# Retention and expert layer on one core: gate matrices loaded by feature, zero products in three gaps

## The chip, the core and the metric

The kernel runs on one core of a Trainium2 chip. The metric is device time in microseconds (us) from start to end of the program; the time before is 446.6 us, the median of three runs (444.99, 446.60 and 446.89 us). A core has five instruction streams that run side by side and wait for each other by semaphores: TensorE (PE) for matrix products, VectorE (DVE), ScalarE (ACT), GpSimd (POOL) and SyncE (SP), which here only issues DMAs.

## The reference

```python
# q, k, v: (4, 8, 768, 64); x of the second part: 3072 tokens x 512 features, 8 experts, F = 1024
state = gamma * state + einsum('bhd,bhe->bhde', k[:, :, t], v[:, :, t])     # for each token t
y[:, :, t] = einsum('bhd,bhde->bhe', q[:, :, t], state) / sqrt(64)
x = y.transpose(0, 2, 1, 3).reshape(3072, 512)
logits = x @ w_gate;  e_idx = argmax(logits, axis=1);  probs = softmax(logits)
eom = 1 / (1 + exp(-(x @ w_output_gate)))
for e in range(8):                                     # each token goes to one expert
    out[e_idx == e] = probs[., e] * eom[., e] * (relu(x[.] @ w1[e]) @ w2[e])
```

Two gate matrices of 512 features by 8 experts are read by the change: `w_gate`, which picks the expert, and `w_output_gate`.

## The kernel before

**Two phases.** The first takes the 3072 tokens in 24 chunks of 128 (four sequences of six), turns them into outputs of the retention, computes their logits, and scatters each token's row into a DRAM buffer sorted by expert. The second runs the experts over that buffer. In the last chunks of the first phase and behind it the largest expert's first 256 rows ("head") are worked off too.

**Order of the work.** In the first phase the order of the instructions of TensorE, VectorE, ScalarE and GpSimd is the order in which they are written; SyncE's DMA queue is ordered by a planner, which mostly keeps the written order. In the second phase TensorE and GpSimd keep the written order.

**A chunk i** (loop L666, `attend` L314) issues on SyncE the loads of key and value chunks i+3 (`load_k`, `load_v`) and, in even chunks, of a query pair (`load_q`); GpSimd scales the value chunk i+2 (`prep_v`, L281, three buffers). TensorE then runs: the scores `s` (L331, 16 products); the product of queries with the state (`py<-qt,sd`, L348; not in a sequence's first chunk); then `between()`: in even chunks from 2 on the logits of the two chunks before (`logits`, L379, which reads `wg`), the transposes of the keys of chunk i+1 (`kt_block`, `pk`, L286), in chunk 1 `spread_gates` (L255), the transposes of the queries of chunk i+2 (`qt_block`, `pq`, L304), and routing; then the products of masked scores with values (`py<-am,vs`, L353) and the state's update (`st`, L361). ScalarE copies the state out as `sd` (L365), VectorE masks the scores into `am` (L335). Key chunks have four buffers: `load_k(i+3)` waits until chunk i-1 has used its buffer.

**The gate matrices.** `wg` is 128 partitions by 4 groups by 32 columns: partition p of group g holds feature 128 g + p, with the two halves of 64 features swapped in groups 2 and 3; columns 0 to 7 belong to `w_gate`, 8 to 15 to `w_output_gate`. GpSimd clears `wg` at the start (L233). ScalarE's queue loads both matrices into `wgs` as 8 rows of 4 KB (L123), ahead of the load of `gv` (L125). In chunk 1, `spread_gates` multiplies them by an identity: 8 products, each shown as two instructions, put them into PSUM by feature, and six copies on VectorE (L257, L259) put them into `wg`. The first reader is `logits(0)` in chunk 2.

**Zero products.** `warm_up(ps, n)` (L138) issues n products of a 128x128 with a 128x512 tile of zeros in bf16; 14 of them stand at the start (L206). The PSUM tiles `pw`, `pg` (decays), `po` (gates) and `misc` (logits) share one buffer.

Of the kernel before, what the change touches and what calls it, by code (L numbers as in the profile page):

```python
# [10 lines left out]
F32 = mybir.dt.float32  # L11
# [21 lines left out]
def retention_moe_kernel(  # L33
# [14 lines left out]
    nc = tc.nc  # L48
    P = 128
    B, H, S, D = q.shape  # L50
    E, DM, DF = w1.shape
# [3 lines left out]
    NG = H // 2  # L55
# [8 lines left out]
    cpool = ctx.enter_context(tc.tile_pool(name="cpool", bufs=1))  # L64
# [53 lines left out]
    nc.scalar.dma_start(dqs, dec_q)  # L118
    dcs = cpool.tile([2, NC * NG], F32, name="dcs")
    nc.scalar.dma_start(dcs, dec_c)  # L120
    wgs = cpool.tile([2 * NG, P * E], F32, name="wgs")
    for j, w in enumerate((w_gate, w_ogate)):
        nc.scalar.dma_start(wgs[j * NG:j * NG + NG], w.rearrange("(g p) e -> g (p e)", p=P))  # L123
    gv = cpool.tile([P, NC, H], F32, name="gv")
    nc.scalar.dma_start(gv, dec_v)  # L125

# [11 lines left out]
    def warm_up(ps, n):  # L138
        for _ in range(n):
            nc.tensor.matmul(ps, wz[:, 0:P], wz, start=True, stop=True)  # L140
# [52 lines left out]
    with ExitStack() as actx:  # L193
# [22 lines left out]
        def load_v(i):  # L216
            b, c = divmod(i, NC)
            vn[i] = ap.tile([P, H, D], F32, name="vn", tag="vn", bufs=4)
            nc.sync.dma_start(vn[i], v[b, :, c * P:(c + 1) * P, :].rearrange("h p d -> p h d"))
# [27 lines left out]
                nc.vector.tensor_copy(gc[:, :, 2 * x:2 * x + 2],  # L247
                                      pm[:, x * NC * NG:(x + 1) * NC * NG].rearrange("p (c g) -> p c g", g=NG)[:, :, 2 * x:2 * x + 2])

        def spread_gates():  # L250

            po = ps_1.tile([P, 512], F32, name="po", tag="misc")[:, 0:2 * NG * E].rearrange("p (e j) -> p e j", e=E)
            wv = wgs.rearrange("j (p e) -> j p e", e=E)
            for e in range(E):
                nc.tensor.matmul(po[:, e], wv[:, :, e], ident[0:2 * NG, 0:2 * NG], start=True, stop=True)  # L255
            for j in range(2):
                nc.vector.tensor_copy(wg[:, 0:2, j * E:j * E + E].rearrange("p g e -> p e g"), po[:, :, j * NG:j * NG + 2])  # L257
                for h in range(2):
                    nc.vector.tensor_copy(wg[h * D:h * D + D, 2:4, j * E:j * E + E].rearrange("p g e -> p e g"),  # L259
                                          po[(1 - h) * D:(2 - h) * D, :, j * NG + 2:j * NG + 4])  # L260

        def more_gq(c):
            nc.gpsimd.tensor_mul(gq[:, c], gq[:, 0],
# [19 lines left out]
        def kt_block(i):  # L283
            pk = ps_t.tile([P, NG, P], F32, name="pk", tag="t")
            for g in range(NG):
                nc.tensor.transpose(pk[:, g], kn[i][:, 2 * g:2 * g + 2].rearrange("p h d -> p (h d)"), ident)  # L286
            kt[i] = ap.tile([P, NG, P], F32, name="kt", tag="kt", bufs=2)
            nc.scalar.copy(kt[i], pk)
# [3 lines left out]
        def qr_block(t):  # L292
            n, r = divmod(t, 2)
            qrs[t] = ap.tile([P, H, D], F32, name="qr", tag="qr", bufs=2)
            (nc.vector.tensor_copy if n == 0 else nc.scalar.copy)(qrs[t], qn[n][:, :, r * D:(r + 1) * D])
# [18 lines left out]
        def attend(i, between, before_state):  # L314
            b, c = divmod(i, NC)
            n, h2 = divmod(i, 2)
            own = slice(64 * h2, 64 * h2 + 64)

            def rm(t):
                return t.rearrange("p (r m) -> p r m", r=2)  # L320

            def qc(r, g):
                return qt[n][r, g, :, own]

            pss = []
            for hh in range(2):
                pss.append(ps_s.tile([P, NG, P], F32, name=f"s{hh}", tag="s"))
            for g in range(NG):
                for hh in range(2):
                    r = slice(hh * 64, hh * 64 + 64)  # L330
                    nc.tensor.matmul(rm(pss[hh][:, g]), kt[i][r, g], qc(r, g), start=True, stop=True)  # L331
            am = []
            for hh in range(2):
                a = ap.tile([P, NG, P], F32, name=f"am{hh}", tag=f"am{hh}", bufs=1)
                nc.vector.tensor_tensor(out=a, in0=pss[hh], in1=mask.unsqueeze(1).broadcast_to([P, NG, P]), op=ALU.mult)  # L335
                am.append(a)

            py = ps_y.tile([P, 2, 512], F32, name="py", tag="y")

            def yo(g, hh):  # L340
                return py[at(g, hh), g // 2, (g % 2) * P:(g % 2) * P + P]

            if c > 0:
                for g in range(2):
                    for gg in (g, g + 2):
                        for hh in range(2):
                            r = slice(hh * 64, hh * 64 + 64)
                            nc.tensor.matmul(rm(yo(gg, hh)), sd[i % 2][r, gg], qc(r, gg), start=(g == 0), stop=False,  # L348
                                             skip_group_check=True)
            between()  # L350
            for g in range(NG):
                for hh in range(2):
                    nc.tensor.matmul(yo(g, hh), vs[i][:, 2 * g + hh], am[hh][:, g],  # L353
                                     start=(c == 0 and g % 2 == 0), stop=True, skip_group_check=True)
            if c < NC - 1:
                if c == 0:
                    rt["st"] = ps_1.tile([P, NG, D], F32, name="st", tag="st")
                st = rt["st"]
                for g in range(NG):
                    for hh in range(2):  # L360
                        nc.tensor.matmul(st[hh * 64:hh * 64 + 64, g], kn[i][:, 2 * g + hh], vs[i][:, 2 * g + hh],  # L361
                                         start=(c == 0 and g == 0), stop=True, skip_group_check=True)
            before_state()
            if c < NC - 1:
                nc.scalar.copy(sd[(i + 1) % 2], st)  # L365
            kn.pop(i), vs.pop(i), kt.pop(i)
            if h2 == 0:
                yts[n] = ap.tile([P, NG, 2, P], F32, name="yt", tag="yt", bufs=2)
            nc.vector.tensor_tensor(out=yts[n][:, :, h2].rearrange("p (x g) t -> p x g t", x=2),
                                    in0=py[:, :, 0:2 * P].rearrange("p x (g t) -> p x g t", t=P),  # L370
                                    in1=gq[:, c].rearrange("p (x g) t -> p x g t", x=2), op=ALU.mult)
# [280 lines left out]
        prep_v(0)  # L652
        prep_v(1)
        kt_block(0)
        qr_block(0)
        qr_block(1)
        qt_block(0)
# [8 lines left out]
        for i in range(NCH):  # L666
            b, c = divmod(i, NC)
            if i + 3 < NCH:
                load_k(i + 3)
                load_v(i + 3)  # L670
            if i == LOAD0:

                n_late = nc.values_load(late[0:1, 0:1], min_val=0, max_val=1)
                with tc.If(n_late > 0):
                    fill(base0, cnt0, 0, HEAD, sm)
                head_load()
# [14 lines left out]
            def between():  # L691
# [3 lines left out]
                    logits(n1)  # L695
                if i + 1 < NCH:
                    kt_block(i + 1)
                if i == 1:
                    spread_gates()
                if 0 < i and i + 2 < NCH:  # L700
                    qt_block(i + 2)
                if i == NCH - 1:
# [5 lines left out]
                if n2 >= 0:  # L708
                    count(n2)
                    misc = rt["misc", n2]  # L710
# [396 lines left out]
```

## Time and profile before

| What | us |
|---|---|
| median of three runs | 446.6 |
| the profiled execution | 447.45 |
| its span, first to last instruction | 445.7 |
| TensorE busy | 429.4 (96%) |
| VectorE busy | 252.9 (57%) |
| ScalarE busy | 191.3 (43%) |
| GpSimd busy | 187.5 (42%) |

The profiled execution's own time is 1.75 us above its span. Times in rows are counted from the span's start. The mean granted TensorE clock over the span was 0.986 of 2.4 GHz. In a timeline, equal neighbouring instructions are merged into one row: start, length from the first start to the last end, engine, line, what it writes and reads, count, and in brackets the idle time before it with what ended it. In a table of windows, the columns are the stretch, its length, the busy time of PE, PE's weight loads, DVE, ACT and POOL (with instructions that start in it), the granted clock as a share of full speed (1.00 is 2.4 GHz, 0.50 is 1.2 GHz), the mean busy share of the DMA engines and GB/s. A line of waits gives the waiting engine, tile and line, what released it, the total, the times and the longest.

### The profile page before, as it was taken

Reading aid. Unit: us, or ns where it says so; the run is one execution under the profiler, and the core shown is the slowest. Engines: PE = TensorE matmul, PEld = TensorE weight load, DVE = VectorE, ACT = ScalarE, POOL = GpSimd, SP = SyncE. Lnnn points to the kernel's source line nnn. Section 1 sums busy time; section 2 is a strip of 40 time slices with the busy share of each in tenths; the row PEclk is TensorE's granted clock in tenths of the full one; section 3 lists DMA queues with packets and bytes.
Section 4 is the critical chain, followed back from the end, with each engine's and each line's share of the span. In section 5 each row is a group of like instructions: output and inputs, shape, how many; then the busy total and the mean of one; then the engine's idle time right before and its main releaser. Section 6 shows DMA issues by size and latency. Waiting matters only on the chain.

```text
span 445.7 us, 9948 instructions
## 1 busy us (share of the span) xinstructions
PE 429.4 (96%) x3586; PEld 394.8 (89%) x3586; DVE 252.9 (57%) x675; ACT 191.3 (43%) x392; POOL 187.5 (42%) x242
## 2 busy tenths in 40 slices
PE   8999999999999998999999999999999999999993
PEld 4888778777877898999999999999999999999882
DVE  1357766766777538564745475476476476476111
ACT  3235555567764223543533453353343453454111
POOL 4433166458988305106005702711730740720722
PEclk9979999999999999899999999999999999999999
DMA  8949999999951277358444834943953863870102
GB/s 199 231 110 259 240 265 300 273 272 245 266 136 73 82 152 212 128 173 212 128 131 136 223 103 136 252 138 103 247 174 95 219 208 96 224 197 4 54 13 71
DMA packets 110068, 75.52 MB, mean 169 GB/s; under 512 B 55459, under 2 KB 97447, under 8 KB 110008
## 3 DMA queue, kind: packets, MB, share of 16 engines
q1 hardware_dynamic: 104720, 62.03, 54.6%
q0 software_dynamic: 5120, 12.69, 8.7%
q8 instruction: 30, 0.49, 0.5%
q14 instruction: 30, 0.25, 0.2%
q10 hardware_dynamic: 168, 0.06, 0.1%
HBM read 59.41 MB, written 15.83 MB: 169 GB/s over the span
## 4 chain that ended last, share of the span: by engine, by line
issue 44%; POOL 14%; PE 3%; DMA 2%; DVE 0%; POOLq 0%
POOL out_dram L185 14%; PE a L627 2%; PE h L609 1%; DMA out_dram<-ot,idi 1%; DMA out_dram<-ot,idx 1%; DVE ot L639 0%; POOLq L185 0%; DVE a L829 0%; DVE tj L802 0%; DVE no L803 0%; POOLq L979 0%
## 5 line engine op out<-in xcount | busy, mean ns | idle before, releaser
L185 POOL DMA_INDIRECT out_dram<-ot,idi x84 | 88.6, 1055 | 157.1 <-DVE ot L901 133.7
L877 PE MATMUL h<-xh,whi 128*128 128x224 f32 (+7 forms) x256 | 86.3, 337 | 0.0
L877 PE MATMUL h<-xw,whi 128*128 128x224 f32 (+7 forms) x256 | 86.2, 337 | 0.0
L877 PE MATMUL h<-xh,wlo 128*128 128x224 f32 (+7 forms) x256 | 86.2, 337 | 0.0
L895 PE MATMUL a<-hh,whi 128*128 128x224 f32 (+6 forms) x224 | 75.5, 337 | 1.1 <-ACT hh L881 1.1
L895 PE MATMUL a<-hl,whi 128*128 128x224 f32 (+6 forms) x224 | 75.7, 338 | 0.3 <-DVE hl L882 0.3
L895 PE MATMUL a<-hh,wlo 128*128 128x224 f32 (+6 forms) x224 | 75.5, 337 | 0.0
L180 DVE TENSOR_TENSOR wlo<-raw,whi 128x512 fp32r<-128x512 f32 x56 | 38.3, 684 | 58.8 <-ACT whi L176 55.8
L176 ACT CAST whi<-raw 128x512 fp32r<-128x512 f32 x64 | 39.8, 621 | 70.7 <-PE a L895 69.0
L882 DVE SCALAR_TENSOR_TENSOR hl<-h,hh 128x224 fp32r<-128x224 f32 (+7 forms) x64 | 34.9, 546 | 55.7 <-ACT hh L881 55.7
L881 ACT ACTIVATE hh<-h 128x224 fp32r<-128x224 f32 (+7 forms) x64 | 30.9, 485 | 79.2 <-PE h L877 79.1
L877 PEld LDWEIGHTS h<-xh,whi 128*128 128x128 f32 x256 | 48.6, 190 | 0.8
L877 PEld LDWEIGHTS h<-xw,whi 128*128 128x128 f32 x256 | 48.5, 190 | 0.7
L877 PEld LDWEIGHTS h<-xh,wlo 128*128 128x128 f32 x256 | 48.5, 189 | 0.5
L895 PEld LDWEIGHTS a<-hh,whi 128*128 128x128 f32 x224 | 42.6, 190 | 1.7 <-ACT hh L881 1.2
L895 PEld LDWEIGHTS a<-hl,whi 128*128 128x128 f32 x224 | 42.6, 190 | 1.0 <-DVE hl L882 0.5
L895 PEld LDWEIGHTS a<-hh,wlo 128*128 128x128 f32 x224 | 42.6, 190 | 0.4
L177 ACT CAST whi<-raw 128x512 fp32r<-128x512 f32 x64 | 39.5, 618 | 0.0
L513 POOL DMA_INDIRECT srt<-row,posi x24 | 24.5, 1019 | 33.4 <-ACT sd L365 11.1
L281 POOL TENSOR_TENSOR vs<-vn,gv 128x512 f32<-128x512 f32 x24 | 25.2, 1049 | 31.4 <-DMA vn<-in_v_dram 16.3
L181 DVE TENSOR_TENSOR wlo<-raw,whi 128x512 fp32r<-128x512 f32 x56 | 38.3, 684 | 0.0
L335 DVE TENSOR_TENSOR am<-s,mask 128x512 f32<-128x512 f32 x48 | 30.9, 686 | 9.8 <-PE s L331 9.8
(168 smaller groups left out, 667.4 us busy)
## 6 DMA issues: line engine op xcount, KB each, us to landing
raw<-in_moe_w_dram SPq DMA_DIRECT2D x32, 512.0 KB
raw<-in_moe_w_dram SPq DMA_DIRECT2D x32, 256.0 KB
raw<-in_moe_w_dram SPq DMA_DIRECT2D x64, 128.0 KB
kn<-in_k_dram SPq DMA_DIRECT2D x24, 256.0 KB
qn<-in_q_dram SPq DMA_DIRECT2D x12, 512.0 KB
vn<-in_v_dram SPq DMA_DIRECT2D x24, 256.0 KB
srt<-zrow SPq DMA_DIRECT2D x8, 325.0 KB
xl<-srt SPq DMA_DIRECT2D x12, 211.2 KB
```

The source lines that it names most:

```text
L176: nc.scalar.copy(cols(hi), r1)
L177: nc.scalar.copy(perm(hi), r2)
L180: eng.tensor_sub(cols(lo), r1, cols(hi).bitcast(F32))
L181: eng.tensor_sub(perm(lo), r2, perm(hi).bitcast(F32))
L185: st = nc.gpsimd.indirect_dma_start(out=dst, out_offset=bass.IndirectOffsetOnAxis(ap=idx, axis=0), in_=src, in_offset=None, bounds_check=n ...
L281: nc.gpsimd.tensor_mul(vs[i], vn.pop(i), gv[:, c, :].unsqueeze(2).broadcast_to([P, H, D]))
L335: nc.vector.tensor_tensor(out=a, in0=pss[hh], in1=mask.unsqueeze(1).broadcast_to([P, NG, P]), op=ALU.mult)
L513: st = nc.gpsimd.indirect_dma_start(out=srt, out_offset=bass.IndirectOffsetOnAxis(ap=posi, axis=0), in_=row, in_offset=None, bounds_check= ...
L877: nc.tensor.matmul(ps[:, 0:C], l[:, 0, w], r[:, dc, 0:C], start=(n == 0), stop=(n == 3 * NDC - 1))
L881: nc.scalar.activation(hh, ps[:, 0:C], AF.Relu)
L882: nc.vector.scalar_tensor_tensor(out=hl, in0=ps[:, 0:C], scalar=0.0, in1=hh.bitcast(F32), op0=ALU.max, op1=ALU.subtract)
L895: nc.tensor.matmul(accs[d][:, 0:C], l[:, 1, w], r, start=(f == 0 and n == 0), stop=(f == NF - 1 and n == 2))
```

## The change

`wgs` and its two loads on ScalarE's queue go, and so do the 8 products and six copies of `spread_gates`. In their place `load_gates` issues six DMAs on SyncE in chunk 0, written behind the loads of the key and value chunks 3 and ahead of the third query pair's: for each matrix one for the first 256 features (128 partitions, 2 runs of 32 bytes each) and two for the swapped halves (64 partitions, 2 runs of 32 bytes each). They write `wg` itself. Beside that, two zero products each are issued at three places of TensorE's order: behind the key transposes of chunk 0 and ahead of its query transposes; in chunk 0 behind the key transposes of chunk 1; in chunk 1 ahead of the state products (L348).

```diff
-    wgs = cpool.tile([2 * NG, P * E], F32, name="wgs")
-    for j, w in enumerate((w_gate, w_ogate)):
-        nc.scalar.dma_start(wgs[j * NG:j * NG + NG], w.rearrange("(g p) e -> g (p e)", p=P))
...
-        def spread_gates():
-
-            po = ps_1.tile([P, 512], F32, name="po", tag="misc")[:, 0:2 * NG * E].rearrange("p (e j) -> p e j", e=E)
-            wv = wgs.rearrange("j (p e) -> j p e", e=E)
-            for e in range(E):
-                nc.tensor.matmul(po[:, e], wv[:, :, e], ident[0:2 * NG, 0:2 * NG], start=True, stop=True)
-            for j in range(2):
-                nc.vector.tensor_copy(wg[:, 0:2, j * E:j * E + E].rearrange("p g e -> p e g"), po[:, :, j * NG:j * NG + 2])
+        def load_gates():
+
+            for j, w in enumerate((w_gate, w_ogate)):
+                x = slice(j * E, j * E + E)
+                nc.sync.dma_start(wg[:, 0:2, x], w[0:2 * P].rearrange("(g p) e -> p g e", p=P))
                 for h in range(2):
-                    nc.vector.tensor_copy(wg[h * D:h * D + D, 2:4, j * E:j * E + E].rearrange("p g e -> p e g"),
-                                          po[(1 - h) * D:(2 - h) * D, :, j * NG + 2:j * NG + 4])
+                    nc.sync.dma_start(wg[h * D:h * D + D, 2:4, x],
+                                      w[2 * P:4 * P].rearrange("(g h p) e -> h p g e", h=2, p=D)[1 - h])
...
+            if i == 1:
+                warm_up(ps_1.tile([P, 512], F32, name="pw", tag="misc"), 2)
             if c > 0:
...
         kt_block(0)
+        warm_up(ps_1.tile([P, 512], F32, name="pw", tag="misc"), 2)
         qr_block(0)
...
                 load_v(i + 3)
+            if i == 0:
+                load_gates()
             if i == LOAD0:
...
                     kt_block(i + 1)
-                if i == 1:
-                    spread_gates()
+                if i == 0:
+                    warm_up(ps_1.tile([P, 512], F32, name="pw", tag="misc"), 2)
                 if 0 < i and i + 2 < NCH:
```

## Rows read from the trace of the kernel before

**Rows 1.** The page, busy time, share of the span and instructions of each engine.
```profile
PE 429.4 (96%) x3586; PEld 394.8 (89%) x3586; DVE 252.9 (57%) x675; ACT 191.3 (43%) x392; POOL 187.5 (42%) x242
```

**Rows 2.** Waits of TensorE, whole span: waiter, releaser, us in total, times, longest.
```profile
PE px L453 <- ACT kt L288: 2.0, 10, 0.2
...
PE misc L460 <- ACT misc L425: 0.2, 1, 0.2
```

**Rows 3.** Timeline of TensorE, start: start us, length us, work [idle before, releaser].
```profile
1.31 5.90 PE L140 MATMUL pw<-wz 128*128 128x512 bf16 x14 [1.31 <-DVE acc L651]
...
8.06 1.09 PE L304 MATMUL pq<-ident,qr 128*128 128x128 f32 x8 [0.42 <-DVE qr L295]
...
12.60 1.49 PE L353 MATMUL py<-am,vs 128*64 128x128 f32 x15 [0.36 <-DVE am L335]
...
16.71 0.67 PE L348 MATMUL py<-qt,sd 64*64 64x128 f32 x16 [0.38 <-ACT sd L365]
...
17.90 3.96 PE L255 MATMUL po<-ident,wgs 8*128 8x8 f32 x16
21.79 1.11 PE L304 MATMUL pq<-ident,qr 128*128 128x128 f32 x4
22.83 1.98 PE L353 MATMUL py<-am,vs 128*64 128x128 f32 x16
24.60 1.07 PE L361 MATMUL st<-vs,kn 128*64 128x64 f32 x16
25.59 1.95 PE L331 MATMUL s<-qt,kt 64*128 64x128 f32 x16
...
28.07 0.64 PE L379 MATMUL misc<-yt,wg 128*32 128x256 f32 x8
```

**Rows 4.** The same timeline, the chunk from 33 us on.
```profile
33.27 0.66 PE L286 MATMUL pk<-ident,kn 128*128 128x128 f32 x4
33.76 0.60 PE L304 MATMUL pq<-ident,qr 128*128 128x128 f32 x4
...
35.19 1.09 PE L353 MATMUL py<-am,vs 128*64 128x128 f32 x16
36.12 0.64 PE L361 MATMUL st<-vs,kn 128*64 128x64 f32 x16
36.68 1.16 PE L331 MATMUL s<-qt,kt 64*128 64x128 f32 x16
```

**Rows 5.** Windows, start: length, busy us by engine, TensorE clock, DMA share, GB/s.
```profile
18.00:20.00 2.00, 2.00 (x9) 2.00 (x9) 0.00 (x0) 0.59 (x1) 0.15 (x1) 1.00 1.19 274
20.00:22.00 2.00, 2.00 (x9) 1.98 (x10) 0.03 (x1) 0.00 (x0) 1.89 (x2) 0.62 1.05 184
22.00:24.00 2.00, 2.00 (x16) 1.67 (x17) 1.07 (x6) 1.06 (x2) 0.00 (x0) 0.50 0.03 7
24.00:26.00 2.00, 2.00 (x28) 1.88 (x26) 0.69 (x1) 0.33 (x2) 0.19 (x1) 0.50 0.00 0
26.00:28.00 2.00, 2.00 (x32) 1.78 (x30) 0.42 (x1) 0.08 (x1) 1.85 (x2) 0.68 0.50 115
```

**Rows 6.** Timeline of SyncE's DMA issues, start: start us, length us, transfer.
```profile
12.98 1.30 SPq L219 DMA_DIRECT2D vn<-in_v_dram  x1
14.39 1.56 SPq L227 DMA_DIRECT2D qn<-in_q_dram  x1
16.05 2.06 SPq L214 DMA_DIRECT2D kn<-in_k_dram  x1
...
25.70 0.37 SPq L214 DMA_DIRECT2D kn<-in_k_dram  x1
```

**Rows 7.** Timeline of GpSimd, start: the scaling of the fourth value tile.
```profile
19.85 1.04 POOL L281 TENSOR_TENSOR vs<-vn,gv 128x512 f32<-128x512 f32 x1 [3.33 <-DMA vn<-in_v_dram]
```

**Rows 8.** Line 155, durations of SyncE's DMA issues: ns min/median/max.
```profile
L155 SPq DMA_DIRECT2D raw<-in_moe_w_dram x64: 598/615/1564, 79.4 to 396.7; - x64
```

**Rows 9.** Windows, from 175 us on.
```profile
175.00:180.00 5.00, 3.60 (x19) 3.23 (x19) 3.85 (x9) 3.37 (x8) 3.96 (x4) 0.75 0.14 45
```

## The prediction, made before the changed kernel had run

> **What bounds the kernel now.** I read the page's busy shares first: TensorE works 96% of the span, every other engine under 60% [rows 1]. Next the waits of TensorE over the whole span. There are ten kinds, from 2.0 us in total (ten times, 0.2 us at most) down to 0.2 us (once), and none was ended by a DMA [rows 2]. So TensorE's own order sets the end, and time taken out of it early should arrive at the end, if no wait takes its place. Then the timeline of TensorE over the first 30 us, where the change sits, and the windows of that stretch. They show two things. From 17.90 to 21.79 us TensorE does nothing but the 16 little products of `spread_gates` [rows 3]. And the granted clock, still 1.00 from 18 to 20 us, is at 0.62 on average from 20 to 22 us, 0.50 from 22 to 26 us and 0.68 from 26 to 28 us [rows 5]: the 1.2 GHz level follows right on that stretch, without any idle of TensorE in these windows (2.00 us busy in each), and lasts through chunk 1 and the scores of chunk 2. I read SyncE's queue and GpSimd's scaling of values last, for what would be late once TensorE comes earlier.
>
> **The products and copies that go.** `spread_gates` starts at 17.90 us and the next work, the query transposes, at 21.79 us: 3.89 us [rows 3]. All of it is on the path: what stands behind it on TensorE waits for nothing in the trace, its inputs being ready. The six copies on VectorE run beside later products, and nobody waits for them but `logits(0)`, which comes much later. The two loads that leave ScalarE's queue stand ahead of work that nobody waits for; I count nothing for them.
>
> **The clock that comes back.** The four groups behind `spread_gates` take 1.11 + 1.98 + 1.07 + 1.95 = 6.11 us [rows 3]; the same four groups in the chunk from 33 us on, at full clock, take 0.60 + 1.09 + 0.64 + 1.16 = 3.49 us [rows 4]. If the fall of the clock was due to the little products, 6.11 - 3.49 = 2.62 us come back. What else could have made it fall? The stretch before 17.90 us has gaps of 0.42, 0.36 and 0.38 us [rows 3], and behind all three the clock is still 1.00 from 18 to 20 us [rows 5], so the removed stretch is the nearest cause. I take the whole 2.62, with 0 as the other end.
>
> A rule of the Trainium skill speaks against that. The page "TensorE: Matmul & The Clock Gate", section "Part 4: PE-mode transpose", says that transposes do not count as work for the clock gate the way ordinary products do, and with the gate products gone, eight transposes stand next to each other in chunk 1. By the rule the clock might fall all the same and the sum below would be 2.62 us less; the chunk from 33 us on has the same eight transposes at full clock [rows 4], which is why I give it a small chance only.
>
> **The zero products.** 14 of them took 5.90 us, 0.42 us each [rows 3], which for 512 columns is the lower level's 1.2 columns per ns; two cost 0.84 us by that row and, at twice the clock, 0.42 us. They go into the three gaps of 0.42, 0.36 and 0.38 us [rows 3], so at full clock they stick out by 0.00, 0.06 and 0.04 us. The second gap covers more than it seems: the products behind it need both halves of `am` and stretch over 1.49 us instead of the 1.09 of a free chunk [rows 3, 4], so a late start there costs nothing. Ends: 0 and, if they ran at the lower level, 3 x 0.84 - 1.16 = 1.36 us. I take 0.1. They wait for no other engine: the PSUM buffer that they share was last read by VectorE's copies of the decays, ahead of the masking that the second gap waits for.
>
> **What is late next in chunk 2.** At full clock, with TensorE further on, the state products of chunk 2 will wait for ScalarE's copy of the state, as those of chunk 1 do for 0.38 us [rows 3]; before, the slow scores covered it. Ends 0 and 0.38; I take 0.1, since ScalarE has the scores' 1.16 us [rows 4] to do it in.
>
> **The six DMAs.** They write 1024 runs of 32 bytes, as many pieces as one key or value load has (1024 of 256 bytes). No row shows such small runs, so I bound them. In the loaded queue, where SyncE goes on as fast as the engines drain it, the issue of 1024 pieces takes 1.30 to 2.06 us (value 3, key 4) [rows 6]; the other end is next to nothing, as there are only 32 KB. The value chunk just ahead of them has landed by 19.85 us, when GpSimd's wait for it ends [rows 7]; the gates land between 19.9 and 21.9 us. `logits(0)` starts at 28.07 us now [rows 3] and would start at about 28.07 - 6.2 = 21.9 us. So the wait is about 0 at either end, and I take 0.1. Behind that wait on TensorE stand the transposes of chunk 2 and everything after. A value below nothing is excluded: an earlier `wg` frees nobody.
>
> By the Trainium skill, "DMA: Bandwidth & Descriptors", section "Specifications", transfers of under 512 bytes a piece are off the full rate; its section "Bandwidth" has a floor of about 10.5 ns per packet, by which 64 pieces on each of 16 engines would be an estimated 0.7 us, inside my bounds.
>
> On SyncE's queue the six stand ahead of query pair 3, key 4 and value 4. An issue of the same kind, half of the partitions with the halves swapped, takes 0.60 to 1.56 us [rows 8]. At 0.60 they hold the queue for 3.6 us, and key 4 is issued by 16.05 + 2.06 + 3.6 = 21.7 us instead of 18.1 [rows 6]. It is needed by the transposes at 33.27 us [rows 4], in future 27.1. Value 3 landed 19.85 - 14.28 = 5.6 us behind its issue with a full queue ahead of it [rows 6, 7]; at that lag key 4 lands at 27.3, but the queue will have emptied meanwhile, and the lag is then shorter. I count 0, with 0.3 as the other end. For key 5 SyncE waits now until 25.70 us, for a buffer [rows 6], and the DMA engines stand still from 22 to 26 us [rows 5]: here lies 4 us of room for the delayed loads.
>
> **The sum.** 3.89 + 2.62 - 0.1 - 0.1 - 0.1 = 6.2 us. The profiled execution would go from 447.45 (span 445.7) to 441.2 us, and the median, 0.85 us below it, from 446.6 to **440.4 us**, 1.4% faster. It is carried to the end because no later wait of TensorE is a DMA's and weight loads follow buffers that TensorE's own progress frees. One thing can move beside it: from 175 to 180 us TensorE is busy 3.60 of 5 us and the clock is at 0.75 on average [rows 9], so half speed for 2.5 us, which costs 1.25 us or somewhat more. Whether that fall comes again when all arrives 6 us earlier the rows cannot tell; without it the time is 439.1.
>
> **Rivals.**
> (a) The clock falls all the same, because of chunk 0's and 1's gaps or the transposes. Against it: the clock was full through the same gaps. Then 3.89 - 0.3 = 3.6 us are left: 443.0 us.
> (b) The loads become the bound. With 1.56 us for each of six issues [rows 8] key 4 is issued by 18.1 + 9.4 = 27.5 us and lands, with half of the full queue's lag of 5.6 us as an estimate, at 30.3, 3.2 us behind its need at 27.1: 443.6 us. For it: the queue is full until 22 us [rows 5]. Against it: the long issues of line 155 are those under a full queue, and its median is 615 ns.
> (c) Slower than before: the little runs themselves. TensorE would stand at `logits(0)` until they land. The gain is used up when they land at 21.9 + 6.2 = 28.1 us, and the kernel is over 0.5% slower from 30.3 us on, that is 10.5 us behind value 3, or 163 ns for each of the 64 runs of a DMA engine, against 20 to 32 ns (1.30 to 2.06 us for 64) of a value's or key's piece [rows 6]. At 200 ns a run they land at 19.85 + 12.8 = 32.7 us, 10.8 us behind their need: 451.2 us. Nothing in the rows points to a factor of five to eight.
> (d) The change doesn't do what it says: SyncE's planner puts the six behind value 4, since nothing ties their place. The DMA engines go idle at 22 us [rows 5], so the six land 1.3 to 2.1 us behind that, at 23.3 to 24.1, and TensorE waits 1.4 to 2.2 us: 442.2 us.
>
> **How the numbers follow.** Forecast 0.68 (a third of it without the later fall of the clock), (a) 0.12, (b) 0.09, (c) 0.04, (d) 0.07. A measurement of this kernel can tell about 0.5%, 2.2 us, from no change: faster means under 444.4. Forecast, (a), (d) and most of (b) are faster: 0.89; the rest of (b) and mild forms of (c) are the same: 0.08; slower 0.03. The range goes from 438.2 (440.4 - 1.25, and 0.9 off for a longer half-speed stretch than the one row shows) to 443.6, which takes in (a), (b) and (d).
>
> **What would show it.** Right: the query transposes of chunk 1 start at about 17.9 us, the windows from 20 to 28 us have clock 1.00, `logits(0)` starts near 21.9 us with under 0.3 us of idle, SyncE's queue has no hole from 22 to 26 us, and every later stage is 6 us earlier. Wrong: a wait of L379 or L286 on a DMA, a clock of 0.50 anywhere before 30 us, or a shift that shrinks between 30 and 160 us.

## The result and the profile after

The changed kernel takes **441.0 us** (median of four runs, 440.45 to 442.21) against 445.8 us for the kernel before in the same sitting (four runs, 444.22 to 446.89): a ratio of 0.990 (95% interval 0.986 to 0.994). A second sitting, with six runs of the changed kernel and eleven of the one before, gave 441.3 against 447.1 us, ratio 0.9875 (0.9845 to 0.9905). Forecast were 440.4 us and a range of 438.2 to 443.6. The profiled execution of after took 440.45 us with a span of 438.7, which is 7.0 us less than the span of before.

On the two chips that ran the first eight experiments every kernel, the one of before included (medians 471.1 and 472.6 us), took some 25 us longer than here, part of it as idle time of TensorE for which the records name no cause, and four of the eight profiled executions (those of the first three experiments and of the gates on ScalarE's queue without the zero products) were among the longer ones of their kernel, so for these eight the verdict is read from the first 30 us of the traces and the ratio only stands beside it.

In the code of after, the same work stands 3 to 6 lines higher: state products L344 (L348 before), key transposes L280 (L286), query transposes L298 (L304), products with values L349 (L353), state update L357 (L361), scores L325 (L331), logits L375 (L379).

The page of after, busy time of each engine and the clock granted in 40 slices of the span:

```profile
PE 422.5 (96%) x3574; PEld 387.7 (88%) x3576; DVE 251.3 (57%) x669; ACT 191.2 (44%) x392; POOL 187.6 (43%) x242
PEclk9999999999999999999999999999999999999997
```

TensorE lost 6.9 us of busy time [rows 1] and is still at 96%: it is the same kernel with a shorter beginning. The timeline of TensorE in after, chunk 1 and the first half of chunk 2, then the state products of chunk 3:

```profile
16.35 0.39 PE L137 MATMUL pw<-wz 128*128 128x512 bf16 x1
16.89 0.67 PE L344 MATMUL py<-qt,sd 64*64 64x128 f32 x16
17.49 0.66 PE L280 MATMUL pk<-ident,kn 128*128 128x128 f32 x4
17.98 0.60 PE L298 MATMUL pq<-ident,qr 128*128 128x128 f32 x4
18.51 1.09 PE L349 MATMUL py<-am,vs 128*64 128x128 f32 x16
19.44 0.63 PE L357 MATMUL st<-vs,kn 128*64 128x64 f32 x16
20.00 1.16 PE L325 MATMUL s<-qt,kt 64*128 64x128 f32 x16
21.09 0.67 PE L344 MATMUL py<-qt,sd 64*64 64x128 f32 x16
21.69 0.64 PE L375 MATMUL misc<-yt,wg 128*32 128x256 f32 x8
...
26.30 0.67 PE L344 MATMUL py<-qt,sd 64*64 64x128 f32 x16 [0.15 <-ACT sd L361]
```

Against [rows 3]: the query transposes start at 17.98 us, right behind the key transposes; the four groups behind take 0.60 + 1.09 + 0.63 + 1.16 = 3.48 us where they took 6.11; and `logits(0)` at 21.69 us has no idle time in front of it. (The pair of zero products at 16.35 us shows one of its two records.) The windows of after, in the columns of [rows 5]:

```profile
18.00:20.00 2.00, 2.00 (x38) 1.77 (x37) 0.27 (x1) 1.59 (x3) 0.91 (x1) 1.00 0.17 13
20.00:22.00 2.00, 2.00 (x44) 1.55 (x40) 1.23 (x3) 0.37 (x1) 1.13 (x2) 1.00 0.36 68
22.00:24.00 2.00, 2.00 (x28) 1.58 (x22) 0.78 (x2) 1.42 (x3) 0.00 (x0) 1.00 1.21 308
24.00:26.00 2.00, 2.00 (x44) 1.89 (x40) 1.82 (x10) 0.74 (x4) 0.00 (x0) 1.00 1.40 224
26.00:28.00 2.00, 1.85 (x30) 1.45 (x26) 1.74 (x6) 0.76 (x3) 1.21 (x2) 1.00 1.10 185
```

The clock is 1.00 all through, and the DMA engines, idle from 22 to 26 us before, are now idle from 18 to 20 us (13 GB/s). SyncE's queue in after shows why. Columns as in [rows 6]; the last number is how many issues the row merges:

```profile
12.85 1.32 SPq L216 DMA_DIRECT2D vn<-in_v_dram  x1
14.28 1.49 SPq L251 DMA_DIRECT2D wg<-in_moe_w_gate_dram  x1
15.81 1.80 SPq L253 DMA_DIRECT2D wg<-in_moe_w_gate_dram  x2
17.66 0.60 SPq L251 DMA_DIRECT2D wg<-n_moe_w_output_gate_dram  x1
18.30 1.25 SPq L253 DMA_DIRECT2D wg<-n_moe_w_output_gate_dram  x2
19.65 0.53 SPq L224 DMA_DIRECT2D qn<-in_q_dram  x1
20.28 0.53 SPq L211 DMA_DIRECT2D kn<-in_k_dram  x1
20.90 1.47 SPq L216 DMA_DIRECT2D vn<-in_v_dram  x1
```

The six gate DMAs hold the queue from 14.28 to 19.55 us, 5.3 us for 32 KB, and what was queued drains behind them. The planner did put them where they are written, behind value 3. The delay reaches GpSimd, which scales value 4 only at 26.80 us in after (25.81 us in before, where TensorE is 6.4 us behind):

```profile
26.80 1.05 POOL L275 TENSOR_TENSOR vs<-vn,gv 128x512 f32<-128x512 f32 x1 [5.66 <-DMA vn<-in_v_dram]
```

TensorE does not feel it. The list of TensorE's waits in after has nine kinds and again no DMA as releaser; here are the one that is new and the smallest (waiter, releaser, total, times, longest):

```profile
PE h L605 <- POOL xw L593: 0.4, 1, 0.4
...
PE misc L456 <- ACT misc L421: 0.2, 1, 0.2
```

How far after is ahead of before, by the start of the same work in the two profiled executions (each value is the time in before less that in after):

| work | ahead by, us |
|---|---|
| scores of chunk 0 (10.49 and 10.58 us) | -0.09 |
| scores of chunk 3 (31.37 and 24.99) | 6.38 |
| scores of chunk 13 (84.64 and 78.25) | 6.39 |
| scores of chunk 23 (137.98 and 131.77) | 6.21 |
| first product of the experts (168.58 and 163.19) | 5.39 |
| last product (438.33 and 431.29) | 7.04 |

So the gain is there by chunk 3, is carried through the first phase, shrinks by 0.82 us between chunk 23 and the experts, and grows by 1.65 us among them. The experiments look at the three parts of the gain first, then at these two steps.

### The profile page after: what moved, and what is told of

It is laid out like the page before. It is cut to its first block, busy times and chain, and to the rows that moved or that the text cites. A ratio compares the mean times of both kernels' runs of the same rounds, so it can differ in the third digit from the quotient of the medians.

```text
span 438.7 us, 9926 instructions
## 1 busy us (share of the span) xinstructions
PE 422.5 (96%) x3574; PEld 387.7 (88%) x3576; DVE 251.3 (57%) x669; ACT 191.2 (44%) x392; POOL 187.6 (43%) x242
## 4 chain that ended last, share of the span: by engine, by line
issue 45%; POOL 14%; PE 3%; DMA 3%; DVE 0%; POOLq 0%
POOL out_dram L182 14%; PE a L623 2%; DMA out_dram<-ot,idi 1%; PE h L605 1%; DMA out_dram<-ot,idx 1%; DVE ot L635 0%; POOLq L182 0%; DVE a L828 0%; DVE tj L801 0%; DVE no L802 0%; POOLq L978 0%
```

## Experiments

For most of them the measure is the time from the first scores (chunk 0) to `logits(0)`: 28.07 - 10.49 = 17.58 us in before, 21.69 - 10.58 = 11.11 us in after. It leaves the start of the kernel out, which varies (see the last section). It also ends where `logits(0)` starts, so a wait inside these logits doesn't show in it; for that their own length (0.64 us in before and in after) has to be looked at.

### The zero products alone, taken out and put in

After without the three pairs:

```diff
-            if i == 1:
-                warm_up(ps_1.tile([P, 512], F32, name="pw", tag="misc"), 2)
             if c > 0:
...
         kt_block(0)
-        warm_up(ps_1.tile([P, 512], F32, name="pw", tag="misc"), 2)
         qr_block(0)
...
-                if i == 0:
-                    warm_up(ps_1.tile([P, 512], F32, name="pw", tag="misc"), 2)
                 if 0 < i and i + 2 < NCH:
```

> The changed kernel without its three pairs of zero products. Theory (the fall of the clock came from the 16 little gate products alone): clock 1.00 in every window from 14 to 28 us, the logits of chunk 0 and 1 start at 21.5 to 21.7 us (21.69 with the pairs), time within 1 us of the changed kernel's 441.0. Rival (the zero products are what holds the clock up): a stretch at 0.50 between 14 and 28 us, these logits at about 24.3 us, time about 443.6.

Measured: 11.01 us from first scores to `logits(0)`, 0.10 less than after, and a granted clock of 1.00 in every window from 14 to 32 us; ratio 0.980 (0.965 to 0.994). The gap stands open again and costs what it cost before. TensorE's timeline of this kernel:

```profile
16.58 0.67 PE L342 MATMUL py<-qt,sd 64*64 64x128 f32 x16 [0.38 <-ACT sd L359]
```

Before with the three pairs added, at the same places (with `spread_gates` left in):

```diff
+            if i == 1:
+                warm_up(ps_1.tile([P, 512], F32, name="pw", tag="misc"), 2)
             if c > 0:
...
         kt_block(0)
+        warm_up(ps_1.tile([P, 512], F32, name="pw", tag="misc"), 2)
         qr_block(0)
...
+                if i == 0:
+                    warm_up(ps_1.tile([P, 512], F32, name="pw", tag="misc"), 2)
                 if i == 1:
```

> The kernel before with the three pairs of zero products and nothing else of the change. Theory: the clock falls as before (0.50 for most of 20 to 27 us), the logits of chunk 0 and 1 start at 28.1 to 28.3 us (28.07 without the pairs), ratio to before 1.000 within the noise. Rival (the zero products hold the clock up): clock 1.00 throughout, these logits at 25.5 us, 2.6 us or 0.6% faster than before.

Measured: 17.60 us, against 17.58 in before; ratio 1.008 (1.002 to 1.014). The windows of this kernel show the same low clock with the gaps filled as without:

```profile
20.00:22.00 2.00, 2.00 (x10) 1.98 (x11) 0.34 (x2) 0.00 (x0) 1.46 (x2) 0.50 0.82 164
...
24.00:26.00 2.00, 2.00 (x28) 1.88 (x26) 0.69 (x1) 0.37 (x1) 0.51 (x1) 0.50 0.00 0
```

The zero products are neither the cause of the gain nor needed for it: they cost 0.1 us and do not hold the clock through the little products.

### The 3.9 us back, without the little products

After with 18 zero products in the place of `spread_gates`, TensorE occupied for the same time by wide work:

```diff
+                if i == 1:
+                    warm_up(ps_1.tile([P, 512], F32, name="pw", tag="misc"), 18)
                 if 0 < i and i + 2 < NCH:
```

> The changed kernel with 18 zero products of 512 columns where the little gate products stood: about as long as those at full clock (18 x 0.216 = 3.9 us), but wide. Theory (3.9 us of work and 2.6 us of clock are two separate terms, and the second goes with the kind of the products): clock 1.00, logits of chunk 0 and 1 at 21.69 + 3.9 = 25.6 us, time 441.0 + 3.9 = 444.9. Rival (the clock falls from the place or from a stretch with no other work): logits at about 28.1 us, time 447.

Measured: 15.00 us, 3.89 more than after, with the clock at 1.00 in every window from 14 to 32 us; ratio 0.992 (0.988 to 0.997). TensorE's timeline:

```profile
16.55 4.05 PE L137 MATMUL pw<-wz 128*128 128x512 bf16 x18
...
24.14 0.64 PE L375 MATMUL misc<-yt,wg 128*32 128x256 f32 x8
```

The two terms of the sum, 3.89 and 2.62 us, are separate: occupying TensorE that long costs the first and leaves the second untouched.

### The little products back, without their loads and copies

After with 16 little products of the same shape (8 products, two instructions each), their weights a row of zeros that lies side by side, no loads and no copies:

```diff
+                if i == 1:
+                    po = ps_1.tile([P, 512], F32, name="po", tag="misc")[:, 0:2 * NG * E].rearrange("p (e j) -> p e j", e=E)
+                    for e in range(E):
+                        nc.tensor.matmul(po[:, e], zrow[0:2 * NG, 0:P], ident[0:2 * NG, 0:2 * NG], start=True, stop=True)
                 if 0 < i and i + 2 < NCH:
```

> The changed kernel with the 8 little products (two instructions each) back at their place, on zeros and with their result unused: no copies on VectorE, no loads of the gates on ScalarE's queue, gates by DMA. Theory (only the products matter): clock at 0.50 for 3 to 7 us from about 20 us on, logits of chunk 0 and 1 at 27.5 to 28.3 us, time as the kernel before, 445 to 447. Rival (part of the gain came from the copies or from the loads' place): the logits come at least 1 us earlier than 27.5 with the same fall of the clock.

The expectation failed. Measured: 13.14 us, 2.03 more than after and not 3.9 or 6.5, and the clock stayed at 1.00; ratio 0.994 (0.990 to 0.999). The same shape took half the time. What differs is how the weights lie: `spread_gates` reads every eighth number of a row, a step of 32 bytes. So the next kernel differs in that (zeros again, no loads, no copies; each product now also reads its own eighth of a row, as in `spread_gates`, where before all eight read the same 128 numbers):

```diff
+    wz8 = cpool.tile([2 * NG, P * E], F32, name="wz8")
+    nc.gpsimd.memset(wz8, 0.0)
+    wz8 = wz8.rearrange("j (p e) -> j p e", e=E)
...
+                if i == 1:
+                    po = ps_1.tile([P, 512], F32, name="po", tag="misc")[:, 0:2 * NG * E].rearrange("p (e j) -> p e j", e=E)
+                    for e in range(E):
+                        nc.tensor.matmul(po[:, e], wz8[:, :, e], ident[0:2 * NG, 0:2 * NG], start=True, stop=True)
```

> The little products on zeros again, now with the weights read 32 bytes apart as in the kernel before (the run with them side by side had 1.95 us for the 16 and kept the clock). Theory (the step of the weights is what made them slow, and with that the clock fall): 16 products in 3.9 to 4.0 us, clock at 0.50 for 3 to 7 us from about 20 us on, logits of chunk 0 and 1 at 27.5 to 28.3 us. Rival (the slowness or the fall came with the copies, the loads of the gates or non-zero data): 16 products in about 2 us, clock 1.00, these logits at 23.7 us.

Measured: 17.41 us against 17.58 in before; ratio 1.000 (0.993 to 1.006). The whole gain is gone, clock included. Line by line, the weight loads of these products (ns min/median/max, first and last start) in before, with side-by-side weights, and with the step of 32 bytes:

```profile
L255 PEld LDWEIGHTS po<-ident,wgs x16: 307/330/331, 17.9 to 21.4; 8*128 8x128 f32 x16
```
```profile
L702 PEld LDWEIGHTS po<-ident,zrow x16: 181/187/187, 17.2 to 18.9; 8*128 8x128 f32 x16
```
```profile
L705 PEld LDWEIGHTS po<-ident,wz x16: 307/330/331, 17.2 to 20.7; 8*128 8x128 f32 x16
```

and TensorE's timeline of the last one, then one of its windows:

```profile
17.18 3.96 PE L705 MATMUL po<-ident,wz 8*128 8x8 f32 x16
21.07 1.11 PE L301 MATMUL pq<-ident,qr 128*128 128x128 f32 x4
22.12 1.98 PE L352 MATMUL py<-am,vs 128*64 128x128 f32 x16
```
```profile
20.00:22.00 2.00, 2.00 (x9) 1.76 (x9) 0.00 (x0) 0.00 (x0) 0.88 (x1) 0.50 0.23 45
```

These are the 3.96, 1.11 and 1.98 us of [rows 3]. Shown, then: the time of `spread_gates` was the time of weight loads at a step, and that run of products alone, without the loads and copies around it, brings the 1.2 GHz level. The same products in 1.95 us do not, nor do 18 wide ones in 4.05 us. Whether the sparse work or its length tips it is open, since the step changes both.

By the Trainium skill, "TensorE: Matmul & The Clock Gate", section "LDWEIGHTS (loading the stationary operand)", a weight load's time is the number of columns over 1.2, an estimated 107 ns for 128 columns; it names no step between them. The rows have 187 and 330 ns for the same 128 columns in f32, and by their first and last start the loads follow each other every 0.11 us with the weights side by side ((18.9 - 17.2) / 15) and every 0.23 us with the step ((20.7 - 17.2) / 15). So the estimate fits the pace of the first and not that of the second; the measurement decides, and where the weights lie counts.

### The gates later, by one chunk

After with the six DMAs behind key and value 4 instead of 3:

```diff
-            if i == 0:
+            if i == 1:
                 load_gates()
```

> The changed kernel with the six gate loads one chunk later, behind value 4 in SyncE's queue. It measures how far the landing of the gates is from being the bound. Prediction's rival (d): TensorE waits 1.4 to 2.2 us at the logits of chunk 0 and 1 (21.7 us), time 442.5 to 443.5. Other theory, from the changed kernel's queue (six issues took 5.3 us from 14.3 to 19.6 us, each behind the landing of earlier loads): the last of the six is issued at about 24 us and lands near 26, so the wait is 3.5 to 5 us and most of the gain is gone, time 444.5 to 446.

Measured: ratio 1.007 (1.001 to 1.013). TensorE's timeline of this kernel:

```profile
24.69 2.25 PE L375 MATMUL misc<-yt,wg 128*32 128x256 f32 x8 [3.69 <-DMA wg<-n_moe_w_output_gate_dram]
```

SyncE's queue in it:

```profile
19.45 1.58 SPq L251 DMA_DIRECT2D wg<-in_moe_w_gate_dram  x1
...
22.50 0.59 SPq L251 DMA_DIRECT2D wg<-n_moe_w_output_gate_dram  x1
23.14 1.25 SPq L253 DMA_DIRECT2D wg<-n_moe_w_output_gate_dram  x2
```

And its windows:

```profile
22.00:24.00 2.00, 0.00 (x0) 0.00 (x0) 0.00 (x0) 0.00 (x0) 0.93 (x1) 0.72 0.17 13
24.00:26.00 2.00, 1.19 (x6) 0.37 (x8) 0.00 (x0) 0.00 (x0) 1.11 (x2) 0.50 0.15 21
```

TensorE stands for 3.69 us, the clock falls to 1.2 GHz, and the logits take 2.25 us instead of 0.64. Not all of that is the clock: of their eight weight loads the first four read the groups 0 and 1, the last four the groups 2 and 3, which the gate DMAs of 64 partitions write, and these last four start 1.2 us behind the first (24.66 us). TensorE's weight loads:

```profile
25.85 0.22 PEld L375 LDWEIGHTS misc<-yt,wg 128*32 128x32 f32 x4 [0.97 <-issue]
```

The last gate DMA, issued from 23.78 us on, is recorded as landed at 25.74 us, so this is a second wait for gates. At half the clock the logits alone would take an estimated 2 x 0.64 = 1.28 us, which leaves some 1.0 us of the 2.25 for it. From first scores to the scores of chunk 3 this kernel needs 30.91 - 9.82 = 21.09 us, after 14.41, before 20.88: of the 6.68 us lost to after 3.69 are the first wait, about 1.0 the second and about 2.0 the slow clock, and the whole gain is gone. The issues took 19.45 to 24.39 us, the last three of them 0.6 us each while the DMA engines were at 0.17 of their time, so there the queue is held by the issues and not by bytes. The last gate landed 2.0 us behind the start of its issue. In after the last issue starts at 18.94 us and its landing is recorded at 21.02 us, 0.7 us ahead of the logits. That is all the margin there is, and the repeat of after, further down, did not have it.

### The gates on ScalarE's queue, with and without the zero products

After with the six DMAs issued on ScalarE at the very start, behind `gv`, into a `wg` that is set up there:

```diff
     nc.scalar.dma_start(gv, dec_v)
+    wg = cpool.tile([P, NG, 32], F32, name="wg")
+    nc.gpsimd.memset(wg[:, :, 2 * E:32], 0.0)
+    for j, w in enumerate((w_gate, w_ogate)):
+        x = slice(j * E, j * E + E)
+        nc.scalar.dma_start(wg[:, 0:2, x], w[0:2 * P].rearrange("(g p) e -> p g e", p=P))
+        for h in range(2):
+            nc.scalar.dma_start(wg[h * D:h * D + D, 2:4, x],
+                                w[2 * P:4 * P].rearrange("(g h p) e -> h p g e", h=2, p=D)[1 - h])
...
-            if i == 0:
-                load_gates()
             if i == LOAD0:
```

> The changed kernel with the same six gate loads on ScalarE's queue at the start, where the two loads of the kernel before stood (the clearing of wg is cut to the columns that no load writes). SyncE's queue is then as before. Theory (the six loads on SyncE cost TensorE nothing): logits of chunk 0 and 1 at 21.4 to 21.9 us, no hole in the DMA traffic from 18 to 20 us, time within 1 us of the changed kernel. Rival (the delayed key and value loads cost something later on, such as the 0.8 us that TensorE loses between 131 and 137 us): TensorE's lead over the kernel before stays at 6.2 us until 170 us and the time is 0.8 us lower.

Measured: 11.11 us, as after; the windows from 10 to 28 us have clock 1.00, and SyncE's hole from 18 to 20 us is gone (268 GB/s there). Ratio 0.991 (0.987 to 0.995). But ScalarE starts its own work late (its first instruction that is not a DMA at 6.55 us, at 2.07 us in after), and TensorE waits for it ahead of the first scores, so that `logits(0)` starts at 22.11 us, later than expected; its timeline:

```profile
9.00 0.66 PE L304 MATMUL pq<-ident,qr 128*128 128x128 f32 x4 [1.14 <-ACT kt L288]
```

From first scores to the scores of chunk 3 this kernel takes 25.41 - 11.00 = 14.41 us, as after. So in this stretch the six loads on SyncE's queue cost TensorE nothing, as the prediction had it, and taking them away from there cost the start 1.14 us of idle time. The part of the rival that lies behind 130 us can't be read here, since there is no trace of before from this chip. The same kernel without the zero products:

> Gate loads on ScalarE's queue at the start and no zero products: the smallest form of the change. Theory (neither SyncE's place nor the zero products matter): logits of chunk 0 and 1 at 21.3 to 21.7 us, clock 1.00 from 14 to 28 us, time within 1 us of the changed kernel. Rival (either matters): the clock falls before 28 us, or these logits start after 22.5 us.

Its edit is the diff above together with that of the first experiment. Measured: ratio 0.984 (0.980 to 0.989), and 11.89 us from first scores to `logits(0)`, which start at 22.86 us; the rival came, the clock fell. TensorE's timeline of this kernel, its window at 12 us, and the same window of the kernel with the zero products:

```profile
8.97 0.66 PE L304 MATMUL pq<-ident,qr 128*128 128x128 f32 x4 [1.70 <-ACT kt L288]
```
```profile
12.00:13.00 1.00, 1.00 (x8) 0.71 (x4) 0.76 (x2) 0.00 (x0) 0.54 (x1) 0.50 1.37 217
```
```profile
12.00:13.00 1.00, 1.00 (x10) 0.58 (x6) 0.73 (x2) 0.21 (x1) 0.49 (x1) 1.00 1.37 218
```

With a gap of 1.70 us and nothing in the others the clock fell at 12 us, with 1.14 us and the pairs it did not: a hint that the zero products guard the clock when a gap grows. It is one execution each, and the ratios don't bear it out (0.991 and 0.984, the wrong way round), so it stays a hint.

### After, and after without the zero products, once more

Both beside before, on a chip where before takes 447.1 us; the first has the edit of the first experiment, the second none.

> The changed kernel without its zero products, beside the changed kernel itself on one chip, for the whole time and for a second look at the clock. Theory (they cost 0.1 us and the clock holds without them here): from the first scores to the logits of chunk 0 and 1 11.0 us, clock 1.00 from 8 to 30 us, whole time within 0.3% of the changed kernel. Rival (they hold the clock in some executions): a stretch at 0.50 before 30 us in this profile, or a whole time over 0.4% above the changed kernel's.

> The changed kernel once more. Theory: logits of chunk 0 and 1 11.1 us behind the first scores, no wait of TensorE for GpSimd's head split (the wait of 0.38 us in the first profile came from one late scatter: 6.2 us from its issue to the head's load, 4.3 to 5.2 in the other traces); ratio to before 0.986 to 0.990. Rival (that wait belongs to the change): it is there again, and the scatter takes about 6 us again.

Measured: without the zero products 440.5 us (six runs, 439.03 to 442.87), ratio 0.9870 (0.9838 to 0.9902); after 441.3 us, ratio 0.9875 (0.9845 to 0.9905). The two can't be told apart. Without the pairs the clock is again 1.00 in every window from 8 to 32 us and the stretch to the start of `logits(0)` takes 11.01 us; with them 11.11, both as in the first two traces.

But the logits themselves take 1.28 us in the repeat of after, twice the 0.64 of its first trace, at a clock of 1.00. TensorE's timeline, its weight loads, and from the list of DMAs the last two gate loads (the last number is the time from issue to landing):

```profile
20.73 1.28 PE L375 MATMUL misc<-yt,wg 128*32 128x256 f32 x8
```
```profile
20.73 0.14 PEld L375 LDWEIGHTS misc<-yt,wg 128*32 128x32 f32 x4 [0.17 <-issue]
21.35 0.17 PEld L375 LDWEIGHTS misc<-yt,wg 128*32 128x32 f32 x4 [0.48 <-issue]
```
```profile
wg<-n_moe_w_output_gate_dram SPq DMA_DIRECT2D x2, 4.0 KB, 2.0
```

In the first trace of after all eight weight loads start within 0.05 us, at 21.69 us. In the repeat the first scores start at 9.62 us instead of 10.58, TensorE is ready for the gates at 20.73 us, and the last gate DMA, issued from 19.19 us on, is recorded as landed at 21.14 us: TensorE waits inside `logits(0)`, 1.28 - 0.64 = 0.64 us, for the gates' DMA. The list of TensorE's waits has no line for it. In the repeat without the zero products the same logits take 0.94 us, from 21.20 us on, and the last gate landed at 21.28 us. So what an execution gains at its start is lost here again: the first scores start at 10.58, 10.19 and 9.62 us in the trace of after and these two, the key transposes behind `logits(0)` at 22.26, 22.08 and 21.94 us. From first scores to the scores of chunk 3 the three take 14.41, 14.62 and 15.05 us, so the change is worth 6.47, 6.26 and 5.83 us there.

The same two traces also settle most of what happened late in the first trace of after. Its 0.82 us lost between chunk 23 and the experts lie at these two waits, which its timeline of TensorE shows:

```profile
133.44 0.67 PE L344 MATMUL py<-qt,sd 64*64 64x128 f32 x16 [0.51 <-ACT sd L361]
...
135.87 0.51 PE L605 MATMUL h<-xw,whi 128*128 128x256 f32 x2 [0.38 <-POOL xw L593]
```

The first was 0.35 us in before, 0.16 less; and the four products on `xw` with the wait among them take 1.13 us (135.09 to 136.22, where the next work starts) instead of the 0.48 us of before (141.13 to 141.61), 0.65 more. `xw` is made from rows that come back from a scatter. From the last scatter's issue to the issue of the load that reads its rows it took 6.23 us in that trace, 5.16 in before and 4.3 to 5.5 in the ten traces of the experiments, none of which has a wait for `xw`. In the repeat of after the lead over before is 6.70 us at chunk 3 (5.83 of the change and 0.87 of the earlier start), 6.41 at chunk 23 and 6.31 at the first product of the experts. So the 0.82 us belong for the most part to that one execution.

The 1.65 us gained among the experts are the later fall of the clock of [rows 9]: in the trace of after it did not come, in the repeat it did. The windows of after, then of its repeat:

```profile
170.00:175.00 5.00, 3.60 (x30) 3.38 (x30) 4.58 (x10) 4.04 (x10) 4.09 (x4) 1.00 0.16 54
```
```profile
170.00:175.00 5.00, 4.49 (x25) 4.30 (x26) 3.92 (x8) 2.79 (x7) 3.79 (x3) 0.71 0.12 39
```

From the first product of the experts to the last it took 269.75 us in before (with the fall), 269.73 in the repeat (with it), 268.10 in after and 268.11 without the zero products (both without it). The fall costs 1.6 us, and it comes or not in executions of the same kernel. Idle time of TensorE for `hh` and its rest stands ahead of it in all four; what decides is open.

## Why the prediction was right, point by point

**The products that go: 3.89 us, right.** The query transposes follow the key transposes at 17.98 us (forecast 17.9), and 18 wide products in their place put back 3.89 us.

**The clock that comes back: 2.62 us, right in size and cause.** Measured 6.11 - 3.48 = 2.63 us. The prediction blamed the little products because the clock was still full behind the three gaps; filling those gaps alone changed nothing, and the little products alone brought the fall back. Rival (a) is out, by the gaps and by the transposes: eight transposes stand together in chunk 1 from 17.49 us on with the clock at 1.00, so the transposes weighed in the prediction did not bring the fall here. (A longer gap did precede a fall: 1.70 us, with the gates on ScalarE's queue and no zero products.) What the prediction did not ask is why 16 products of 8 columns took 3.9 us; the answer is how their weights lie.

**The zero products: 0.1 us, right.** 11.11 against 11.01 us, twice.

**Waits in chunk 2: 0.1 us each, too much in one execution, too little in two.** In the first trace of after the state products of chunk 2 (21.09 us) and `logits(0)` (21.69 us) start without idle time, and the next chunk's state products wait 0.15 us. In the repeats the wait for the gates is 0.64 us, and 0.30 without the zero products. The forecast 6.2 us was 6.47 us from first scores to `logits(0)`, less 0.09 us at the start.

**SyncE's queue: mis-sized, without effect on key 4, but not on the gates.** The term was 6 x 0.6 = 3.6 us from the median of line 155; it measured 5.3 us. Three issues of the six took 0.6 us each as forecast (0.60, and 1.25 for two), into near-idle DMA engines; the first three stood in a queue still full (1.49, and 1.80 for two), 1.1 us each. Key 4 was issued all the same by 20.28 + 0.53 = 20.8 us, ahead of the forecast 21.7, because its own issue and that of the query pair took 0.53 us each in the drained queue instead of 2.06 and 1.56 [rows 6]. Rival (b), with 1.56 us for each of the six and a late key 4, did not come about. But the last gate was issued 5.3 - 3.6 = 1.7 us later than by this term; without that the gates of the repeat would have landed at an estimated 21.14 - 1.7 = 19.4 us, ahead of their reader. The hole of the DMA engines did not vanish, it moved from 22 to 26 us to 18 to 20 us.

**The landing of the gates: inside its bounds, but "the wait is about 0 at either end" was not right.** The last gate landed at 21.02 us (forecast 19.9 to 21.9), 0.7 us ahead of its reader. The step took the reader's 21.9 us as fixed; it moves with the start of the kernel, and in the repeat it came at 20.73 us, with the landing at 21.14. That is the prediction's own sign of being wrong, a wait of the logits on a DMA, and in small what rival (c) describes. That it cost only 0.64 us there, and nothing in the first trace, is luck as far as the working goes. The size of (c), 163 ns a run and more, is out: the last DMA landed 2.0 us behind its issue in the late version and in the repeat. Whether the small runs make these 2.0 us no run shows.

**Rival (d): right as a mechanism, its price far too low.** The planner did keep the written place, but the late version shows what it would have cost: 3.69 us of waiting ahead of the logits and about 1.0 us inside them, not 1.4 to 2.2, and about 2.0 us of low clock that the working had not counted. The forecast of 442.2 us for this case should have been no gain at all. Two steps of it failed. The wait ran from 21.0 us (forecast need 21.9) to 24.69 us, and the last gate landed at 25.74 us (forecast 24.1 at the latest); and the clock was left out, though the prediction knew from [rows 5] what a low one costs.

**Carried to the end: right, with two errors that offset each other.** The lead of 6.38 us lost 0.17 us by chunk 23 and 0.82 us in one execution's wait for `xw`, which the prediction excluded ("no later wait of TensorE is a DMA's": GpSimd's rows came by one); the later fall of the clock did not return in this execution, 1.65 us where 1.25 "or somewhat more" was forecast. In the repeat the wait for `xw` did not come and the fall did, and the last product comes 438.33 - 432.00 = 6.3 us earlier than in before. That this meets the forecast 6.2 is in part luck too: 0.87 us of it is the earlier start, and 0.64 us went at the gates.

The difference of the medians, 4.8 and 5.8 us in the two sittings, is less than 6.3 us, but the intervals of both (0.9857 to 0.9941 of 446 us are 2.6 to 6.4 us; 0.9845 to 0.9905 of 447 us are 4.2 to 6.9 us) take it in. One sum of the chances is loose: the forecast, (a) and (d) make 0.87, so 0.89 for faster leaves 0.02 of (b)'s 0.09, which is not most of it.

## What to carry to other kernels

A run of tiny products costs what its weight loads cost, so look at how the weights lie before you count columns; and a sparse run on TensorE can cost a second time, at the clock of what follows, so price it from the same work elsewhere at full clock. A load that replaces on-chip work is free only as long as it lands ahead of its reader: move it by one chunk in a trial, read the landing and the reader's own length in more than one execution to see the margin, and charge a missed one for the clock as well as for the wait. Small DMAs are charged to the queue that issues them by their number, not their bytes: in the drained queue a gate load of 4 or 8 KB took 0.6 us to issue, a key load of 256 KB 0.53 us.

## What the runs showed that was not expected

- A weight load of 8 x 128 in f32 takes 187 ns with the columns side by side and 330 ns at a step of 32 bytes; the products follow at 0.12 and 0.25 us each (1.95 and 3.96 us for 16).
- Six DMAs of 32 KB together held SyncE for 5.3 us in after and 4.9 us in the late version: 0.6 us for an issue beside near-idle DMA engines, up to 1.6 us in a full queue.
- A landing that is late by one chunk cost 6.68 us: 3.69 us of waiting ahead of the logits, about 1.0 us inside them, about 2.0 us through the clock.
- The gate loads land at 21.02 to 21.28 us in the trace of after, its repeat and the repeat without zero products, whether TensorE is ready for them or not, and cost it nothing, 0.64 and 0.30 us.
- The start of the kernel varies: 14 warm-up products took 4.58 to 6.16 us over the twelve traces, and the first key transposes began at 5.72 to 7.26 us. In after all 14 start 0.42 us apart, in the repeat the first nine do and the last five 0.21 us apart, so what varies is when they reach their full pace. The fall of the clock among the experts adds 1.6 us or not. Together that is about the spread of the times of one kernel, and about half of what this change is worth.
